# The last two blocks' input projection moved from behind dense 1 to inside it

## The chip, the cores and the metric

The kernel runs on one core of one Trainium2 chip. The metric is the time of one execution on the device in microseconds (us), as the median of several runs. PE is TensorE (matmuls), DVE is VectorE, ACT is ScalarE, POOL is GpSimd, and SP is the sync engine, which here issues most DMAs. PSUM is the memory into which PE accumulates; it has 8 banks of 128 x 512 fp32.

## The reference, cut to what matters

A state-space layer (S5) and a dense layer with mish read the same normalised input, and both results are added to the input:

```python
def _A_ref(x, Lambda_re, Lambda_im, B_re, B_im, C_re, C_im, log_dt, Dskip):
    Lam_bar = jnp.exp(dt * Lam)                                # dt = exp(log_dt)
    B_bar = ((Lam_bar - 1.0) / Lam)[:, None] * Bmat
    Bu = jnp.einsum("bld,pd->blp", x + 0j, B_bar)              # input projection
    for t in range(L):
        h = Lam_bar[None, :] * h + Bu[:, t, :]                 # recurrence
    y = 2.0 * jnp.einsum("blp,dp->bld", hseq, Cmat).real + x * Dskip[None, None, :]

def _B_ref(x, w1, b1, w2):
    h = jnp.einsum("bsd,df->bsf", x, w1) + b1                  # dense 1
    act = h * jnp.tanh(sp)                                     # sp = softplus(h): mish
    return jnp.einsum("bsf,fd->bsd", act, w2)                  # dense 2

xn = _layernorm(x, axis=-1)
return x + _A_ref(xn, ...) + _B_ref(xn, ...)
```

There are 2048 rows, 1024 columns and 1024 complex states, and 3584 hidden columns in the dense layer. Inputs and output are bf16.

## The kernel before, in words

The 2048 rows are cut into four blocks of 512 (`blk` 0 to 3 in the code; "blocks 3 and 4" of the change are `blk` 2 and 3, those with `blk >= FAST`). Rows 512 at a time stand in the free axis of `xnT`, the transposed normalised input. Each block goes through these stages on PE:

- **Dense 1**: 28 weight tiles `f`, each 8 matmuls of 512 columns (L777) into one PSUM bank, bank `f % 8`. DVE takes each tile out of its bank with one bias addition (L786) into `hb`. This is the tile's evacuation.
- **Input projection**: in `blk` 2 and 3 it is `project_fast`, a Strassen-like scheme with seven products for each of four pairs of state tiles, called `a` to `d`. A product (L830) is 8 matmuls of 256 columns. `ORDER` names products and what stands between them, in the order in which they are issued. For each pair the products use three banks X, Y and Z: 4, 5, 6 for `a` and `c`, and 0, 1, 2 for `b` and `d`. Products 1, 2 and 5 open a bank; 6, 7 and 4 add to what product 1 left in X, and 3 adds to what 5 left in Z. Before a bank is added to, its state has to be copied out. These copies ("snaps", L845 on DVE for `a` and `b`, L847 on ACT for `c` and `d`) go to SBUF, and additions of a bank and a snap ("joins", L855 on DVE) make the results. PE may issue `a6` only when DVE has done the snap of `a1`, `b6` only behind the snap of `b1`, and `a3` only behind the snap of `a5`. A last copy follows product 4 (L872 on DVE, L874 on ACT).
- **Dense 2 and output projection** (`tail`, both L956): eight accumulation units, one for each bank, take 28 hidden tiles and then the state tiles. In `blk` 2 and 3 the units 7, 5, 6 and 4 take the first six hidden tiles among the last products (the `u` entries in `ORDER`), as banks come free.

All instructions of an engine run in the order in which the Python code issues them. A helper (`Queue`) puts a semaphore wait in front of each instruction that reads or overwrites another engine's work.

Beside the stages run: on ACT the three passes of mish for each group of 7 tiles (`mish(g)`, L755 to L757), issued behind tiles 6, 13, 20 and 27; on DVE the product `mish_mul(g)` (L762), issued ahead of the evacuations of tiles 14 and 21 for groups 0 and 1, and at the `m` entries of `ORDER` for 2 and 3. Also on DVE: `ln_skip` behind tiles 8, 10, 12 and 15 (L516, L518); in `blk` 2 the eight calls of `sums_B` (four operations each, L1124 and L1126), which make the summed weights of the products; `rotate_in` (the `r` entries, L796 to L801); the layer norm of the next block; and `recur` (the recurrence). POOL makes the summed inputs with `sums_x` (L1131), each behind an `ln_skip`. SP loads weights into a ring of 7 slots (L375) as slots come free, and issues the transposes of the next block (L522), which are queued among the loads of dense 2.

Of the kernel before, what the change touches and what calls it, by code (L numbers as in the profile page):

```python
# [163 lines left out]
def build_kernel(nc, A_x, A_Lambda_re, A_Lambda_im, A_B_re, A_B_im, A_C_re, A_C_im,  # L164
# [6 lines left out]
    NB = S // TB  # L171
# [3 lines left out]
    NF = F // P  # L175
# [3 lines left out]
    assert S % TB == 0 and D == 1024 and NP == 1024 and NF == NG * GF and NQ == 4  # L179
    EPS = 1e-5  # L180
    FAST = 2

    PE = Queue(nc, "pe")
    VE = Queue(nc, "ve")
# [8 lines left out]
    NRING = 7  # L193
# [565 lines left out]
    def mish_mul(g):  # L759
        hs = hb[:, (g % 2) * GF:(g % 2) * GF + GF, :]  # L760
        a = act[:, g * GF:(g + 1) * GF, :]
        vop(lambda e: e.tensor_tensor(a, a, hs, op=ALU.mult), reads=[b_act[g], b_hb[g % 2]], writes=[b_act[g]])  # L762
# [6 lines left out]

    def first_tile(blk, f):  # L770
        bank, hs = f % 8, f % (2 * GF)
        raw = blk == 0 and f < NR
        if raw:
            first_rest(f)
        for k in range(0 if raw else NK):
            s, w = w1_tile(n_item[0], f % 4, k)
            PE.mm(lambda e, k=k, w=w: e.matmul(ps[:, bank, :], lhsT=w, rhs=xnT[:, k, :],  # L777
                                               start=k == 0, stop=k == NK - 1),
                  reads=[b_ring[s]] + b_xnT, writes=[b_ps[bank]], first=k == 0, last=k == NK - 1)
        if f % 4 == 3:  # L780
            item_done()
            item_done()
        if f % GF == 0 and f >= 2 * GF:
            mish_mul(f // GF - 2)
        ts = slice(2 * P if raw else 0, 4 * P)
        vop(lambda e: e.tensor_scalar(hb[:, hs, ts], ps[:, bank, ts], b1(f), None, op0=ALU.add),  # L786
            reads=[b_ps[bank], b_par], writes=[b_hbf[hs]])
        if f % GF == GF - 1:
            mish(f // GF)
# [4 lines left out]
    def rotate_in(j):  # L794
        for s in range(2):
            vop(lambda e, s=s: e.tensor_tensor(  # L796
                mt[:, s, :, :], hT16[:, :, j, :], tab[:, s, j, :].unsqueeze(1).to_broadcast([P, 2, TB]), op=ALU.mult),
                reads=[b_hT[0][j], b_hT[1][j], b_tab[j]], writes=[b_m[s]])
        vop(lambda e: e.tensor_tensor(hT[:, 0, j, :], mt[:, 0, 0, :], mt[:, 1, 1, :], op=ALU.add),
            reads=b_m, writes=[b_hT[0][j]])  # L800
        vop(lambda e: e.tensor_tensor(hT[:, 1, j, :], mt[:, 0, 1, :], mt[:, 1, 0, :], op=ALU.subtract),  # L801
            reads=b_m, writes=[b_hT[1][j]])
# [3 lines left out]
    def product(pr, n):  # L806

        X, Y, Z = (4 * ((pr + 1) % 2) + i for i in range(3))
        js = (2 * pr, 2 * pr + 1)
        lo, hi = slice(0, TH), slice(TH, TB)  # L810
        raw = {1: (0, 0, lo), 2: (0, NH, lo), 4: (1, NH, None), 3: (None, NH, hi)}
        bank = {1: X, 6: X, 7: X, 4: X, 2: Y, 5: Z, 3: Z}[n]
        opens = n in (1, 2, 5)
        for j in js:
            for k in range(NH):
                if n in (1, 2, 4):
                    w = BT[:, raw[n][0], j, raw[n][1] + k, :]
                    b_w = b_BT[j]
                elif n == 7:
                    w, b_w = BT16[:, 1, j, k, :], b_BT[j]  # L820
                else:
                    w, b_w = SS[:, j, {5: 0, 6: 1, 3: 2}[n], k, :], b_CT[j]
                if n in (1, 2, 3):
                    x, b_x = xnT[:, raw[n][1] + k, raw[n][2]], b_xnT
                else:
                    t = {5: 0, 6: 1, 7: 2, 4: 3}[n]
                    x, b_x = TT[:, t, k, :], [b_xn[t]]
                o = (j - js[0]) * TH
                begin, end = j == js[0] and k == 0, j == js[1] and k == NH - 1
                PE.mm(lambda e, w=w, x=x, o=o, begin=begin, end=end: e.matmul(  # L830
                    ps[:, bank, o:o + TH], lhsT=w, rhs=x, start=opens and begin, stop=end, skip_group_check=True),
                    reads=[b_w] + b_x, writes=[b_ps[bank]], first=begin, last=end, chained=not opens)

    def evacuate(pr, n, keep):
# [34 lines left out]
        if n == 4:  # L869
# [3 lines left out]
            else:  # L873
                aop(lambda e: e.copy(dst, bank(X)), reads=[b_ps[X]], writes=b_hT[1][j0:j0 + 2])  # L874

    ORDER = ("a2 a1 b2 b1 a5 b5 a6 b6 a3 b3 a7 b7 c2 d2 a4 b4 c5 c1 r0 d5 d1 r1 c6 c3 d6 d3 "
             "c7 d7 u7 c4 r2 u5 d4 u6 u4 r3 r4 r5 r6 r7 m2 m3")

    def project_fast(open_unit):
        keep = {}  # L880
        for o in ORDER.split():
            kind, n = o[0], int(o[1])
            if kind == "r":
                rotate_in(n)
            elif kind == "u":
                open_unit(n)
            elif kind == "m":
                mish_mul(n)
            else:
                product("abcd".index(kind), n)  # L890
                evacuate("abcd".index(kind), n, keep)

    def project_in(blk):
        for j in range(NJ):
# [55 lines left out]
    def tail(blk):  # L950
# [8 lines left out]
        def dense(f, s, units):  # L959
            wt = ring[:, s, :].rearrange("p (f d) -> p f d", f=2)  # L960
            for u in units:
                q, h = u // 2, u % 2
                acc(u, act[:, f, q * P:(q + 1) * P], wt[:, f % 2, h * TB:(h + 1) * TB], [b_actf[f], b_ring[s]],
                    tell=f % 2 == 1 and u == 7)

        base_items = [0]

# [17 lines left out]
        njt = 1 if blk == 0 else 3  # L985
        base = n_item[0]

        def open_unit(u):
            for f in range(6):
                dense(f, (base + f // 2) % NRING, (u,))  # L990

        yield open_unit
        if blk < FAST:
            for f in range(6):
                dense(f, (base + f // 2) % NRING, (4, 5, 6, 7))
        for f in range(NF):
            dense(f, (base + f // 2) % NRING, (0, 1, 2, 3) if f < 6 else range(8))
            if f % 2 == 1:
                item_done()
            if blk + 1 < NB and f in (9, 11, 13, 15):  # L1000
                transpose_dma((f - 9) // 2)
# [30 lines left out]
        for q in range(NQ):  # L1032
            units = (2 * q, 2 * q + 1) if not (ends and q == NQ - 1) else (2 * q,)
# [122 lines left out]
    for blk in range(NB):  # L1156
        def side(f):
            if blk:
                if f in (8, 10, 12, 15):
                    ln_skip(blk, (8, 10, 12, 15).index(f))  # L1160
                    if blk >= FAST:
                        sums_x((8, 10, 12, 15).index(f))
                if blk == FAST and f in (1, 2, 4, 5, 17, 19, 22, 24):
                    sums_B((1, 2, 4, 5, 17, 19, 22, 24).index(f))
                return
            if f == 13:
                for j in range(NJ):
                    table(j)
            if f in (5, 6, 7, 8):
                coefficients(f - 5)  # L1170
            if f in (8, 9, 11, 12):
                ln_skip(0, (8, 9, 11, 12).index(f))
            if f in (14, 16, 18, 20):
                ln_stats_only(1, (f - 14) // 2)
            if f < 24 and f % 3 == 2:
                transpose_B(f // 3)
            if f >= 26:
                transpose_C(f - 26)

        for f in range(NF):  # L1180
            first_tile(blk, f)
            side(f)
        out_stage = tail(blk)
        open_unit = next(out_stage)
        if blk >= FAST:
            project_fast(open_unit)
        else:
            project_in(blk)
        if 0 < blk < NB - 1:
            for q in range(NQ):  # L1190
                ln_stats_only(blk + 1, q)
            ln_rsqrt()
            for q in range(NQ):
                ln_scale(blk + 1, q)
        if blk:
            next(out_stage)
        for j in range(NJ):
            recur(blk, j)
            if blk == FAST - 1:
                prepare(j)  # L1200
            if blk:
                continue
            if j == 0:
                mish_mul(3)
                ln_root()
                for q in range(NQ):
                    ln_scale(1, q)
                next(out_stage)
            scale_C(j)
        if blk + 1 < NB:  # L1210
            carry()
        if blk == FAST - 1:
            vop(lambda e: e.tensor_tensor(qi[:], qi[:], c("ss").unsqueeze(1).to_broadcast([P, 2, NJ]), op=ALU.mult),
                reads=[b_qi, b_cs["ss"]], writes=[b_qi])
            rows_spread()
            for j in range(NJ):
                scale_B(j)
        for _ in out_stage:
            pass
        if blk == FAST - 1:  # L1220
            snaps_ready()
# [36 lines left out]
```

## Time and profile before

| What | Value |
|---|---|
| Time before, median of 3 runs (lowest, highest) | 614.18 us (614.16, 614.73) |
| The profiled execution: its own time | 614.87 us |
| Its span in the profile | 613.6 us |
| Granted TensorE clock | 1.0 in all slices |
| Busy: PE, DVE, ACT, POOL | 609.6, 502.2, 289.9, 83.3 us |
| Dense 1 of `blk` 2, of `blk` 3 begins | 313.94, 462.72 us |
| Products of `blk` 2, of `blk` 3 begin | 362.29, 511.06 us |

Times within the profile are counted from the start of the span. A line of a timeline gives the start, the length, the engine, the line of the kernel, the operation, output and input, the number of instructions that are merged into the line, and, in square brackets, the idle time in front of it and what ended it. "x3" with a length of 2.18 us is three instructions that followed each other without a pause; the distance of their starts is less than the length of one, because the end of one overlaps the next. The chain of waits is followed back from the last instruction of the kernel, and a piece of it gives start, length, engine and line.

### The profile page before, as it was taken

To read this page: it belongs to the slowest core of one execution; us is meant where nothing else is said; L and a number is where in the kernel's file an instruction comes from. 1 tells how busy PE (TensorE), PEld (TensorE's weight loads), DVE (VectorE), ACT (ScalarE), POOL (GpSimd) and SP (SyncE) were. 2 spreads that over 40 slices of the span, in tenths; PEclk is the share of its full clock that TensorE was granted. 3 is DMA by queue.
4 is the path that set the end of the run, shared out by engine and by line. 5 is a ranking of instruction groups with operands and counts; after the bars stand their busy time and mean duration, and the time that the engine had idled before them with its cause. 6 is when DMAs were issued, how large, how long until landed. Compare 5 with 4: busy or idle time off the path is not lost.

```text
span 613.6 us, 8046 instructions
## 1 busy us (share of the span) xinstructions
PE 609.6 (99%) x3151; PEld 306.9 (50%) x3151; DVE 502.2 (82%) x796; ACT 289.9 (47%) x217; POOL 83.3 (14%) x83
## 2 busy tenths in 40 slices
PE   8999999999999999999999999999999999999998
PEld 7644444444444444444444468544444447844444
DVE  6989999999557599999968886999954776799923
ACT  4589998332059952724605998000000999400000
POOL 2899200000100001300013300000000510000000
PEclk9999999999999999999999999999999999999999
DMA  9999984950355401997545530059446443016421
GB/s 233 291 246 301 222 166 133 259 158 0 117 160 171 170 2 52 308 296 223 237 139 160 181 138 1 1 177 275 160 140 209 138 152 123 1 41 235 170 71 69
DMA packets 102768, 97.02 MB, mean 158 GB/s; under 512 B 51722, under 2 KB 81034, under 8 KB 102730
## 3 DMA queue, kind: packets, MB, share of 16 engines
q1 hardware_dynamic: 96688, 80.56, 45.7%
q0 software_dynamic: 2352, 7.61, 3.9%
q10 hardware_dynamic: 3690, 8.34, 3.6%
q8 instruction: 25, 0.41, 0.3%
q14 instruction: 13, 0.11, 0.1%
HBM read 76.04 MB, written 8.39 MB: 138 GB/s over the span
## 4 chain that ended last, share of the span: by engine, by line
PE 98%; DMA 1%; SPq 0%; DVE 0%; issue 0%
PE ps L956 49%; PE ps L777 30%; PE ps L898 9%; PE ps L830 8%; PE ps L582 1%; PE ps L591 1%; DMA ring<-in_B_w_dram 1%; PE ps L981 0%; PE ps L434 0%; SPq L343 0%; PE ps L469 0%; DVE xx L1046 0%; SPq L339 0%; PE ps L617 0%
## 5 line engine op out<-in xcount | busy, mean ns | idle before, releaser
L956 PE MATMUL ps<-ring,act 128*128 128x512 bf16 x896 | 194.7, 379 | 0.0
L777 PE MATMUL ps<-xnT,ring 128*128 128x512 bf16 x840 | 182.0, 379 | 0.0
L956 PEld LDWEIGHTS ps<-ring,act 128*128 128x128 bf16 x896 | 87.7, 98 | 104.5
L777 PEld LDWEIGHTS ps<-xnT,ring 128*128 128x128 bf16 x840 | 82.2, 98 | 98.9
L755 ACT ACTIVATE act<-hb 128x3584 bf16<-128x3584 bf16 x16 | 50.9, 3183 | 125.7 <-DVE hb L786 125.5
L786 DVE TENSOR_SCALAR hb<-ps,par 128x512 bf16<-128x512 f32 (+1 forms) x112 | 79.2, 728 | 37.4 <-PE ps L777 36.5
L921 DVE TENSOR_TENSOR_SCAN hT<-cs,qi,hT 128x512 bf16<-128x512 f32 x48 | 58.9, 1268 | 0.0
L898 PE MATMUL ps<-xnT,BT 128*128 128x512 bf16 x256 | 55.6, 379 | 0.0
L956 PE MATMUL ps<-CT,hT 128*128 128x512 bf16 x256 | 55.6, 379 | 0.0
L956 PE MATMUL ps<-ring,hT 128*128 128x512 bf16 x250 | 54.3, 379 | 0.0
L757 ACT ACTIVATE act<-act 128x3584 bf16<-128x3584 bf16 x16 | 51.0, 3190 | 0.2
L756 ACT ACTIVATE act<-act 128x3584 bf16<-128x3584 bf16 x16 | 51.0, 3190 | 0.2
L926 DVE TENSOR_TENSOR mt<-hT,tab 128x1024 bf16<-128x1024 bf16 x64 | 41.4, 688 | 1.1
L903 DVE TENSOR_TENSOR mt<-ps,tab 128x1024 bf16<-128x1024 f32 x32 | 37.7, 1219 | 5.0 <-PE ps L898 3.9
L898 PEld LDWEIGHTS ps<-xnT,BT 128*128 128x128 bf16 x256 | 25.1, 98 | 30.2
L956 PEld LDWEIGHTS ps<-CT,hT 128*128 128x128 bf16 x256 | 25.0, 98 | 30.2
L956 PEld LDWEIGHTS ps<-ring,hT 128*128 128x128 bf16 x250 | 24.4, 98 | 29.5
L762 DVE TENSOR_TENSOR act<-act,hb 128x3584 bf16<-128x3584 bf16 x16 | 34.1, 2144 | 3.3 <-ACT act L757 3.3
L1023 DVE TENSOR_TENSOR xx<-ps,xx 128x1024 bf16<-128x1024 f32 (+1 forms) x16 | 18.8, 1189 | 22.0 <-PE ps L956 21.9
L1131 POOL TENSOR_TENSOR TT<-xnT 128x1024 f16<-128x1024 bf16 x4 | 10.3, 2582 | 146.7 <-DVE mt L516 146.7
L1077 ACT ACTIVATE hb<-hb 128x1024 bf16<-128x1024 bf16 x16 | 16.7, 1046 | 23.1 <-DMA hb<-in_A_B_re_dram 13.5
L1108 ACT ACTIVATE act<-CT,cs 128x2048 bf16<-128x2048 bf16 x7 | 14.0, 2002 | 22.1 <-DVE cs L1091 19.7
(142 smaller groups left out, 578.9 us busy)
## 6 DMA issues: line engine op xcount, KB each, us to landing
ring<-in_B_w_dram SPq DMA_DIRECT2D x112, 512.0 KB, 4.5
ring<-ctd SPq DMA_DIRECT2D x16, 512.0 KB, 3.2
out_dram<-xx ACTq DMA_DIRECT2D x15, 256.0 KB, 2.0
ctd<-act ACTq DMA_DIRECT2D x7, 512.0 KB, 3.8
xx<-in_A_x_dram POOLq DMA_DIRECT2D x12, 256.0 KB, 3.9
hb<-in_A_B_re_dram POOLq DMA_DIRECT2D x8, 256.0 KB, 4.0
hb<-in_A_B_im_dram POOLq DMA_DIRECT2D x8, 256.0 KB, 4.1
xx<-in_A_x_dram SPq DMA_DIRECT2D x3, 256.0 KB, 5.9
```

Source lines behind the costliest of these rows:

```text
L755: aop(lambda e: e.activation(a, hs, AF.Exp), reads=[b_hb[g % 2]], writes=[b_act[g]])
L756: aop(lambda e: e.activation(a, a, AF.Ln, bias=1.0), reads=[b_act[g]], writes=[b_act[g]])
L757: aop(lambda e: e.activation(a, a, AF.Tanh), reads=[b_act[g]], writes=[b_act[g]])
L762: vop(lambda e: e.tensor_tensor(a, a, hs, op=ALU.mult), reads=[b_act[g], b_hb[g % 2]], writes=[b_act[g]])
L777: PE.mm(lambda e, k=k, w=w: e.matmul(ps[:, bank, :], lhsT=w, rhs=xnT[:, k, :], start=k == 0, stop=k == NK - 1), reads=[b_ring[s]] + b_xnT, ...
L786: vop(lambda e: e.tensor_scalar(hb[:, hs, ts], ps[:, bank, ts], b1(f), None, op0=ALU.add), reads=[b_ps[bank], b_par], writes=[b_hbf[hs]])
L830: PE.mm(lambda e, w=w, x=x, o=o, begin=begin, end=end: e.matmul(ps[:, bank, o:o + TH], lhsT=w, rhs=x, start=opens and begin, stop=end, ski ...
L898: PE.mm(lambda e, j=j, ci=ci, k=k, bank=bank: e.matmul(ps[:, bank + ci, :], lhsT=BT[:, ci, j, k, :], rhs=xnT[:, k, :], start=k == 0, stop= ...
L903: vop(lambda e, s=s, u=u, j=j: e.tensor_tensor(mt[:, s, :, :], u, tab[:, s, j, :].unsqueeze(1).to_broadcast([P, 2, TB]), op=ALU.mult), rea ...
L921: vop(lambda e, ci=ci, init=init: e.tensor_tensor_scan(out=hT[:, ci, j, :], data0=cj("r", j).to_broadcast([P, TB]), data1=hT[:, ci, j, :], ...
L926: vop(lambda e, s=s: e.tensor_tensor(mt[:, s, :, :], hT[:, :, j, :], tab[:, s, j, :].unsqueeze(1).to_broadcast([P, 2, TB]), op=ALU.mult), ...
L956: PE.mm(lambda e: e.matmul(ps[:, u, :], lhsT=lhsT, rhs=rhs, start=st_, stop=last), reads=reads, writes=[b_ps[u]], first=st_, last=last, te ...
```

## The change

In `blk` 2 the products are issued behind dense 1's tile 21, in `blk` 3 behind tile 15 (`SPLIT` 22 and 16 counts the tiles ahead). Two tiles stand among the last products, the others behind them (`f` in `ORDER` and `REST`). All of dense 2 comes behind tile 27: the `u` entries are gone, and four units take the first six hidden tiles, then the other four. The tiles use banks in an order of their own. `mish_mul(3)` moves on DVE from the end of `ORDER` to behind the first state tile of `recur`. In `blk` 2 the last five calls of `sums_B` move to earlier tiles.

```diff
+    SPLIT = {blk: 22 if blk == FAST else 16 for blk in range(FAST, NB)}
...
     def first_tile(blk, f):
         bank, hs = f % 8, f % (2 * GF)
+        if blk >= FAST:
+            f0 = f - SPLIT[blk]
+            bank = (EARLY_BANKS if f0 < 0 else LATE_BANKS)[f0 % 8]
...
+    EARLY_BANKS = (5, 1, 4, 0, 6, 2, 3, 7)
+    LATE_BANKS = (7, 3, 5, 1, 6, 2, 4, 0)
     ORDER = ("a2 a1 b2 b1 a5 b5 a6 b6 a3 b3 a7 b7 c2 d2 a4 b4 c5 c1 r0 d5 d1 r1 c6 c3 d6 d3 "
-             "c7 d7 u7 c4 r2 u5 d4 u6 u4 r3 r4 r5 r6 r7 m2 m3")
-
-    def project_fast(open_unit):
+             "c7 d7 f c4 f d4 ")
+    REST = {16: "f r2 f f r3 f f r4 f f r5 f f f r6 r7 m2", 22: "f r2 f r3 f r4 f r5 r6 r7 m2"}
+
+    def project_fast(tile, f):
         keep = {}
-        for o in ORDER.split():
+        for o in (ORDER + REST[f]).split():
...
+            if kind == "f":
+                tile(f)
+                f += 1
...
             for u in units:
                 q, h = u // 2, u % 2
                 acc(u, act[:, f, q * P:(q + 1) * P], wt[:, f % 2, h * TB:(h + 1) * TB], [b_actf[f], b_ring[s]],
-                    tell=f % 2 == 1 and u == 7)
+                    tell=f % 2 == 1 and u == units[-1])
...
+        opens, rest = (4, 5, 6, 7), (0, 1, 2, 3)
+        if blk >= FAST:
+            opens, rest = ((7, 4, 3, 0), (5, 1, 6, 2)) if SPLIT[blk] == 22 else ((6, 2, 4, 0), (7, 3, 5, 1))
+        for f in range(6):
+            dense(f, (base + f // 2) % NRING, opens)
         for f in range(NF):
-            dense(f, (base + f // 2) % NRING, (0, 1, 2, 3) if f < 6 else range(8))
+            dense(f, (base + f // 2) % NRING, rest if f < 6 else range(8))
...
-                if blk == FAST and f in (1, 2, 4, 5, 17, 19, 22, 24):
-                    sums_B((1, 2, 4, 5, 17, 19, 22, 24).index(f))
+                if blk == FAST and f in (1, 2, 4, 6, 11, 14, 17, 19):
+                    sums_B((1, 2, 4, 6, 11, 14, 17, 19).index(f))
...
-        for f in range(NF):
+        def tile(f):
             first_tile(blk, f)
             side(f)
-        out_stage = tail(blk)
-        open_unit = next(out_stage)
+
+        for f in range(SPLIT.get(blk, NF)):
+            tile(f)
         if blk >= FAST:
-            project_fast(open_unit)
+            project_fast(tile, SPLIT[blk])
         else:
             project_in(blk)
+        out_stage = tail(blk)
...
-        if blk:
+        if 0 < blk < FAST:
             next(out_stage)
         for j in range(NJ):
             recur(blk, j)
+            if blk >= FAST and j == 0:
+                mish_mul(3)
+                next(out_stage)
```

More of the change, by code (lines that the diff above doesn't have):

```diff
@@ L874, in evacuate @@
                 aop(lambda e: e.copy(dst, bank(X)), reads=[b_ps[X]], writes=b_hT[1][j0:j0 + 2])
+    EARLY_BANKS = (5, 1, 4, 0, 6, 2, 3, 7)
+    LATE_BANKS = (7, 3, 5, 1, 6, 2, 4, 0)
     ORDER = ("a2 a1 b2 b1 a5 b5 a6 b6 a3 b3 a7 b7 c2 d2 a4 b4 c5 c1 r0 d5 d1 r1 c6 c3 d6 d3 "
-             "c7 d7 u7 c4 r2 u5 d4 u6 u4 r3 r4 r5 r6 r7 m2 m3")
-    def project_fast(open_unit):
+             "c7 d7 f c4 f d4 ")
+    REST = {16: "f r2 f f r3 f f r4 f f r5 f f f r6 r7 m2", 22: "f r2 f r3 f r4 f r5 r6 r7 m2"}
+    def project_fast(tile, f):
         keep = {}
-        for o in ORDER.split():
[L882 to L886, printed above, removed]
+        for o in (ORDER + REST[f]).split():
+            kind = o[0]
+            if kind == "f":
+                tile(f)
+                f += 1
+            elif kind == "r":
+                rotate_in(int(o[1]))
             elif kind == "m":
-                mish_mul(n)
+                mish_mul(int(o[1]))
             else:
-                product("abcd".index(kind), n)
-                evacuate("abcd".index(kind), n, keep)
+                product("abcd".index(kind), int(o[1]))
+                evacuate("abcd".index(kind), int(o[1]), keep)
+        assert f == NF
     def project_in(blk):
@@ L986, in tail @@
         base = n_item[0]
[L988 to L995, printed above, removed]
+        opens, rest = (4, 5, 6, 7), (0, 1, 2, 3)
[3 more added lines that the diff above has]
+            dense(f, (base + f // 2) % NRING, opens)
         for f in range(NF):
-            dense(f, (base + f // 2) % NRING, (0, 1, 2, 3) if f < 6 else range(8))
+            dense(f, (base + f // 2) % NRING, rest if f < 6 else range(8))
             if f % 2 == 1:
```

## The prediction

> **What bounds the kernel now.** I read the page's busy table first: PE is busy 609.6 of 613.6 us. Busy is not proof of full rate, so next came the chain of waits (start, length, engine and line):
>
> ```profile
> 313.94 48.35 PE ps L777 x224
> 362.29 22.71 PE ps L830 x208
> 385.00 1.29 PE ps L956 x6
> 386.29 0.87 PE ps L830 x8
> 387.17 1.29 PE ps L956 x6
> 388.46 0.87 PE ps L830 x8
> 389.33 73.38 PE ps L956 x340
> ```
>
> Each piece starts where the last one ends. A 512-column matmul costs 48.35/224 = 0.2158 us and a 256-column one 22.71/208 = 0.1092 us, in every piece of `blk` 2 and 3. So there is no hole in PE's stream to close. The change leaves every matmul in place and only reorders them: it can gain nothing on PE, and whatever makes PE wait is lost for good. The question is only whether PE must now wait for a bank, a snap or an activation.
>
> Next, DVE's timeline around the place where the products begin, and one SS group (`sums_B`) and one POOL operation ahead of it:
>
> ```profile
> 344.88 2.56 POOL L1131 TENSOR_TENSOR TT<-xnT,TT 128x1024 f16<-128x1024 bf16 x1 [4.39 <-DVE mt L516]
> ...
> 346.70 1.03 DVE L1124 TENSOR_TENSOR SS<-BT 128x512 f16<-128x512 bf16 x1
> 350.35 0.41 DVE L1124 TENSOR_TENSOR SS<-BT 128x512 f16<-128x512 bf16 x1
> 360.90 2.18 DVE L786 TENSOR_SCALAR hb<-ps,par 128x512 bf16<-128x512 f32 x3
> 364.07 0.69 DVE L845 COPY snaps<-ps 128x512 f32<-128x512 f32 x1 [0.99 <-PE ps L830]
> 364.80 0.69 DVE L855 TENSOR_TENSOR hT<-ps,snaps 128x512 f16<-128x512 f32 x1
> ```
>
> At tile 28 DVE has caught up and even waits 0.99 us for the first snap. But behind tile 21 (evacuated at 356.16, when PE had left it at about 351.9) DVE is over 4 us late. The new order starts the products exactly there. The same operation takes 1.03 us at 346.70 and 0.41 at 350.35: at 346.70 POOL's sum runs until 347.44, and DVE ends 0.29 later. In `blk` 3 a `mish_mul` shows it more strongly:
>
> ```profile
> 486.63 2.63 POOL L1131 TENSOR_TENSOR TT<-xnT 128x1024 f16<-128x1024 bf16 x1 [0.82 <-DVE mt L516]
> ...
> 487.86 3.29 DVE L762 TENSOR_TENSOR act<-act,hb 128x3584 bf16<-128x3584 bf16 x1
> 500.20 2.02 DVE L762 TENSOR_TENSOR act<-act,hb 128x3584 bf16<-128x3584 bf16 x1 [0.44 <-ACT act L757]
> ```
>
> It ends 1.89 us behind POOL's end (489.26): nearly its whole 2.02 us lie behind POOL. A DVE operation with two SBUF inputs thus waits until POOL's running sum is over.
>
> **The change, part by part. DVE in `blk` 2.** Nothing moves ahead of tile 10's evacuation (332.98) but the fourth SS group, from behind tile 5 to behind tile 6, into a hole of 0.53 us. From there I add DVE's queue up in its new order, by distances of starts in the trace: an evacuation 0.66 (two in 1.32 at 342.73 to 344.05), an `ln_skip` 1.33, an SS group 1.72, a `mish_mul` 2.13. An SS group caught behind POOL ends 1.58 after POOL's end (349.02 - 347.44), a `mish_mul` 1.99 after it (491.25 - 489.26). POOL's sum ends 4.05 us after the evacuation ahead of its `ln_skip` begins (332.98 to 337.03).
> - Tile 10 and skip: 334.97. Tile 11: 335.63. SS group 5, now here, meets POOL until 337.03: 338.61.
> - Tile 12 and skip: 340.60. POOL starts late too and runs to 342.67. Tile 13: 341.26. `mish_mul(0)` waits for POOL: 344.66.
> - Tile 14 and SS group 6: 347.04. Tile 15 and skip: 349.03, POOL until about 351.05. Tiles 16, 17: 350.35. SS group 7 waits for POOL: 352.63.
> - Tiles 18, 19 and SS group 8: 355.67. Tile 20: 356.33. `mish_mul(1)`: 358.46. Tile 21: **359.12**.
>
> None of this waits for PE or ACT: ACT's first mish ends at about 339, the second at 353.5 (12.1 us each by 328.37 to 340.47).
>
> **PE meets it.** Without stalls the products start at 313.94 + 22 x 1.727 = 351.93, one each 0.873: `a6` at 357.17, `b6` at 358.04, `a3` at 358.91. The six products ahead of `a6` need banks 5, 4, 1, 0, 6, 2, last used by tiles 14 to 19 and empty by 354: no wait. DVE's snaps follow tile 21 (0.73 for a snap with its join behind, 0.61 for the join, 0.65 for snaps in a row, a length of 0.69): snap `a1` ends 359.81, `b1` 361.15, `a5` 362.49. So with 0.06 for the signal (DVE's first operation ends at 0.98, PE starts at 1.04) `a6` starts at 359.87, 2.70 late; `b6` adds 0.47, `a3` 0.47. `a3` starts at 362.55 instead of 358.91: **3.64 us**. Behind it the line is clear: `a7` starts 0.5 us behind its snap, `c5` is ready at 370.4 and ACT's mish, begun at about 356.5, is over by 368.6.
>
> Each restart may also pay for a weight load; the rows give 98 ns, and only the last restart counts: 0.1 us, between 0 and 0.1.
>
> **The rest of `blk` 2.** PE ends tile 27 at T = 390.4. The last six evacuations stand among `r` entries; tile 27's ends at T + 3.8, needed at T + 5.8, when the second four units begin (24 matmuls ahead of them). `m2`: T + 12, needed at tile 14 of dense 2, T + 24. Then the layer norm (11.1 us by 402.75 to 413.85), one `recur` (4.5) and `mish_mul(3)` (2.1): T + 30; ACT's third pass is over at T + 16; needed at tile 21, T + 36. The next block's transposes wait on SP for the norm, until T + 23, in front of weight loads for tile 24 of dense 2 (T + 41); before, they were issued at 412.60 to 418.97, some 10 us ahead of that tile. All hidden, with 2 us of cover at the least; if one is late, PE pays what is over.
>
> **`blk` 3** has no SS groups. DVE's queue up to tile 15 is unchanged and ends with the skip at 493.90; products start at 490.35. Snap `a5` ends at 497.27, `a3` starts at 497.33: cover zero, cost 0 to 0.1; I take 0.05. Its two joins ahead fall in POOL's last sum (to 495.96); if they were held as above, `a3` would be 1.3 late. They read one input from PSUM, and L599, of that kind, keeps its 0.42 us at 19.23 with POOL busy, so I take 0. Behind tile 27 (T), its evacuation is done at T + 1.7, `m2` at T + 8, `mish_mul(3)` at T + 16: covered.
>
> Sum: 3.64 + 0.1 + 0.05 = 3.8 us. Against the profiled execution's own 614.87 (span 613.6 and 1.27 around it) that is 618.7; against the median, 0.69 lower, 618.0.
>
> **A clock penalty.** PE has never stood still for 2.7 us in this trace. The nearest rows: at the start 128-column matmuls run at 0.107 us (18 in 2 us) and only from 6.57 at 0.055, so the array runs at half rate in its first 5.5 us; a pause of 0.83 us at 7.07 does not bring that back (56 of 257 columns in 6.18 us, 0.110 each). So the price of the new pause lies between 0 and 5.5/2 = 2.75 us; I take 0, the row of the pause being of the same kind.
>
> The Trainium skill ("TensorE: Matmul & The Clock Gate", "Why this matters for your kernels") says that matmul bursts shouldn't lie more than about 3 us apart, or the array drops to half clock; no row here shows it. By that rule 2.70 us just passes and the sum stays 3.8; a stall 0.3 us longer would break it, so the rule speaks against this change.
>
> **The rivals.**
> 1. *DVE is not held by POOL* (the two long rows have another cause). Then tile 21 is out 3.1 us earlier, at 356.03; `a6` finds its snap done, `a3` starts 0.55 late: 614.18 + 0.55 + 0.1 = 614.8, no measurable change. Against it: both rows end by POOL's end, and four `mish_mul`s without POOL beside them take 2.02. Chance 0.10.
> 2. *The pause trips the clock*: 3.8 plus up to 2.75, less what later stalls (0.94) absorb: about 619 to 620.6. For it: 2.7 us is three times the longest pause shown. Chance 0.10.
> 3. *A later wait* (dense 2's second units, `mish_mul(3)`, or `blk` 3's joins): 0.5 to 2 us more, 618.5 to 620. For it: covers of 2 us and zero. Chance 0.09.
> 4. *Faster*: only if PE's stream held waits that the trace hides. At 0.2158 us for all 224 matmuls of a piece, a hidden stop has no room. Chance 0.02.
>
> The forecast itself, 617.3 to 618.6, has 0.69. A measurement of this kernel can tell about 0.2%, 1.2 us, from no change. Faster 0.02, same 0.10 (rival 1), slower 0.88. The range takes rivals 2 and 3 in, up to 620.6, and below it reaches to one of the three POOL waits (1.27, 1.26, 0.56) or two being absent: 618.0 - 2.2 = 615.8.
>
> **What would show it.** In the profile after: PE waits at L830 for DVE L845, three in `blk` 2, the longest about 2.7 us, some 3.6 in all; tile 21's evacuation ends near 359.2; SS groups 5 and 7 and `mish_mul(0)` stretched behind POOL; no PE wait in `blk` 3 over 0.1; the granted clock and 0.109 us for each product matmul unchanged. The prediction is wrong if `a6` starts by 358 or if waits appear at L956.

## The result, and the profile after

| | Kernel before | Changed kernel |
|---|---|---|
| Median (lowest to highest), 4 runs each | 614.34 us (614.16 to 614.73) | 619.59 us (618.12 to 621.16) |
| Ratio to before, 95% interval | | 1.0085 (1.0059 to 1.0111) |
| Profiled execution, its span | 614.87, 613.6 us | 620.03, 618.6 us |
| Mean granted clock | 1.0 | 0.997 in three of the four, 1.0 in the run of 618.12 |

The kernel became 5.25 us slower. The forecast was 618.0 us with a range from 615.8 to 620.6. The one run with an undisturbed clock took 618.12.

The chain of waits of the changed kernel (start, length, engine and line; L790, L763, L849 and L859 are before's L786, L762, L845 and L855, and L834 the products) shows where PE's unbroken stream of before is cut:

```profile
314.06 19.01 PE ps L781 x88
...
358.59 0.75 DVE hb L790
...
360.66 0.61 DVE snaps L849
361.27 0.05 issue
361.32 18.14 PE ps L834 x152
...
391.56 75.97 PE ps L965 x352
...
495.16 22.84 PE ps L834 x208
```

Before, the chain was PE alone from 22 us on. Now it leaves PE behind tile 10 (333.07) and runs through DVE's queue up to the snap of `b1`; only `b6`, at 361.32, takes it back. Two lengths are also new. The 152 product matmuls from there take 18.14 us, where 152 x 0.1092 is 16.60. And the 208 of `blk` 3 take 22.84 instead of 22.71: the 0.13 us at `a3`. Behind 391.56 all other pieces have before's lengths.

PE's timeline around the products, and its only wait behind the kernel's start in the waits (total, times, longest):

```profile
355.38 1.91 PE L834 MATMUL ps<-TT,SS 128*128 128x256 f16 x16
359.99 3.21 PE L834 MATMUL ps<-TT,SS 128*128 128x256 f16 x16 [2.70 <-DVE snaps L849]
```

```profile
PE ps L834 <- DVE snaps L849: 2.7, 1, 2.7
```

`a5` and `b5` take 1.91 us; PE stands still for 2.70; then `a6` and `b6`, of the same size, take 3.21 with one short wait for the snap of `b1` (in PE's row it is hidden behind the weight load, whose own row waits 0.56 us). The windows (PE, weight load, DVE, ACT and POOL busy, then the granted clock) say why:

```profile
core 0: us, PE busy (x) PEld busy (x) DVE busy (x) ACT busy (x) POOL busy (x), PEclk, DMA share, GB/s
...
357.20:359.90 2.70, 0.09 (x1) 0.00 (x0) 2.59 (x3) 2.68 (x2) 0.00 (x0) 1.00 0.00 0
359.90:361.00 1.10, 1.01 (x8) 0.70 (x8) 1.07 (x3) 1.10 (x1) 0.00 (x0) 0.89 0.00 0
361.00:362.00 1.00, 0.88 (x5) 0.50 (x5) 0.96 (x3) 0.99 (x2) 0.00 (x0) 0.50 0.00 0
...
364.00:365.00 1.00, 1.00 (x11) 0.84 (x10) 0.73 (x2) 0.98 (x2) 0.00 (x0) 0.92 0.00 0
```

The pause runs at full clock; 0.77 us behind it the clock drops to 0.50 (0.89 over 1.10 us: half for the last 0.24) and is back 0.16 us behind 364.00. That is 3.40 us of half rate.

DVE's timeline in the same stretch:

```profile
335.75 1.68 DVE L1130 TENSOR_TENSOR SS<-BT 128x512 f16<-128x512 bf16 x1
...
341.38 3.29 DVE L763 TENSOR_TENSOR act<-act,hb 128x3584 bf16<-128x3584 bf16 x1
...
350.46 1.02 DVE L1130 TENSOR_TENSOR SS<-BT 128x512 f16<-128x512 bf16 x1
...
356.47 2.01 DVE L763 TENSOR_TENSOR act<-act,hb 128x3584 bf16<-128x3584 bf16 x1
358.59 0.75 DVE L790 TENSOR_SCALAR hb<-ps,par 128x512 bf16<-128x512 f32 x1
```

POOL's timeline, with the three sums they meet:

```profile
334.59 2.56 POOL L1137 TENSOR_TENSOR TT<-xnT,TT 128x1024 f16<-128x1024 bf16 x1 [0.89 <-DVE mt L517]
340.15 2.63 POOL L1137 TENSOR_TENSOR TT<-xnT 128x1024 f16<-128x1024 bf16 x1 [3.00 <-DVE mt L517]
348.64 2.56 POOL L1137 TENSOR_TENSOR TT<-xnT,TT 128x1024 f16<-128x1024 bf16 x1 [5.86 <-DVE mt L517]
```

SS groups 5 and 7 and `mish_mul(0)` are stretched just where the prediction put POOL's sums (0.41 to 1.68 and 1.02, and 2.02 to 3.29): the SS operations end 0.28 us behind POOL's end, `mish_mul(0)` 1.89. Tile 21's evacuation begins at 358.59 and the snap behind it at 359.26. Summed in advance was 359.12, in a time that began 0.12 earlier.

### The profile page after: what moved, and what is told of

It is laid out like the page before. It is cut to its first block, busy times and chain, and to the rows that moved or that the text cites. A ratio compares the mean times of both kernels' runs of the same rounds, so it can differ in the third digit from the quotient of the medians.

```text
span 618.6 us, 8053 instructions
## 1 busy us (share of the span) xinstructions
PE 611.4 (99%) x3151; PEld 306.5 (50%) x3151; DVE 503.7 (81%) x796; ACT 290.6 (47%) x217; POOL 84.9 (14%) x83
## 4 chain that ended last, share of the span: by engine, by line
PE 94%; DVE 5%; DMA 1%; SPq 0%; issue 0%; DVEq 0%
PE ps L965 49%; PE ps L781 26%; PE ps L907 9%; PE ps L834 7%; DVE hb L790 1%; DVE SS L1130 1%; PE ps L583 1%; PE ps L592 1%; DMA ring<-in_B_w_dram 1%; DVE act L763 1%; DVE xx L519 0%; DVE mt L517 0%; DVE BT L1132 0%; PE ps L990 0%; DVE snaps L849 0%; PE ps L435 0%
## 5 line engine op out<-in xcount | busy, mean ns | idle before, releaser
L790 DVE TENSOR_SCALAR hb<-ps,par 128x512 bf16<-128x512 f32 (+1 forms) x112 | 79.5, 729 | 38.3 <-PE ps L781 37.3
L763 DVE TENSOR_TENSOR act<-act,hb 128x3584 bf16<-128x3584 bf16 x16 | 35.5, 2219 | 2.9 <-ACT act L758 2.9
L340 POOL DMA_DIRECT2D xx<-in_A_x_dram x12 | 6.7, 559 | 129.0 <-DVE xx L1029 124.6
```

## The experiments

The theory was: DVE's queue in `blk` 2, lengthened by SS groups put ahead of the products and by waits for POOL, is late with the snap of `a1`; PE stands still; and the pause trips the clock in some executions. The rivals were a cost of the move itself (late evacuations, `mish_mul(3)`, `blk` 3), and a clock or a scatter that has nothing to do with the pause.

The start of the kernel scatters. In these profiles `blk` 2 begins anywhere from 312.8 to 314.6 us (a wait of its own in e1 left out), behind code that no kernel here changes, and the kernel before takes 613.85 to 616.62 us over three sets of runs. So besides the times I give, as **loss in `blk` 2**, the distance from dense 1's first matmul to dense 2's first in PE's timeline, less 72.80 us for 224 matmuls of 0.2158 and 224 of 0.1092. For the changed kernel it is 391.40 - 313.90 - 72.80 = 4.70.

| Kernel | Median us | Before, run beside it | Ratio, 95% interval | Clock below 1.0 | Loss in `blk` 2 |
|---|---|---|---|---|---|
| a1_after_again | 620.15 | 614.20 | 1.0095 (1.0077 to 1.0112) | 5 of 6 | 4.55 |
| e11_fill_3 | 620.07 | 614.53 | 1.0092 (1.0078 to 1.0105) | 4 of 6 | 3.75, clock 1.0 |
| e6_fill_half | 618.40 | 614.20 | 1.0070 (1.0058 to 1.0082) | 0 of 5 | 3.78 |
| e2_fill_pause | 618.65 | 614.73 | 1.0064 (1.0052 to 1.0077) | 0 of 5 | 3.78 |
| e3_split24 | 616.56 | 614.73 | 1.0026 (1.0015 to 1.0037) | 0 of 7 | 1.63 |
| e5b_no_pool | 615.30 | 614.53 | 1.0017 (1.0008 to 1.0025) | 0 of 12 | 0.61 |
| e8_split26_reordered | 614.98 | 614.53 | 1.0008 (0.9997 to 1.0019) | 0 of 10 | 0.01 |
| e7_blk3_alone | 614.76 | 614.20 | 1.0010 (0.9999 to 1.0021) | 0 of 12 | |
| e1_blk3_only | 617.22 | 614.73 | 1.0037 (1.0024 to 1.0051) | 0 of 5 | own waits |
| e4_split26 | 624.16 | 614.73 | 1.0149 (1.0135 to 1.0163) | 4 of 4 | own waits |

### Which block pays

**e1_blk3_only.** `blk` 2 is put back behind all 28 tiles, but inside the new code:

```diff
-    SPLIT = {blk: 22 if blk == FAST else 16 for blk in range(FAST, NB)}
+    SPLIT = {2: 28, 3: 16}
...
-                if blk == FAST and f in (1, 2, 4, 6, 11, 14, 17, 19):
+                if blk == FAST and f in (1, 2, 4, 5, 17, 19, 22, 24):
```

> In blk 2 the products stand behind all 28 tiles again and the SS groups at their old tiles; blk 3 is as in the changed kernel. Theory (the whole loss is DVE's late queue in blk 2 and the clock after PE's pause): 614.3 to 614.6 us, executions as close together as those of the kernel before, no PE wait for a snap in blk 2, at most 0.15 us at a3 of blk 3. Rival (the new order costs something in blk 3 too, in dense 2's units or mish_mul(3)): 615 us or more, with PE waits behind 460 us.

Neither came true as meant: 2.5 us were lost, and two waits that this version brought with it, 1.41 and 0.81 us in `blk` 2, make most of it. PE's timeline:

```profile
315.45 1.89 PE L781 MATMUL ps<-xnT,ring 128*128 128x512 bf16 x8 [1.41 <-DVE xx L1029]
```

```profile
387.47 1.92 PE L834 MATMUL ps<-TT,BT 128*128 128x256 f16 x16 [0.81 <-DVE hT L859]
```

With 28 as the split, the bank list gives tile 0 bank 6, which the block before frees last. And without tiles (or, in the old code, `u` units) between `d7` and `c4`, `c4` comes before DVE has joined `c7`. It undoes the change only in name, so it says nothing on `blk` 3.

**e7_blk3_alone** restores the old order of `blk` 2 with its banks and units (`project_old` goes through the `ORDER` of before):

```diff
+    SPLIT = {3: 16}
...
-        if blk >= FAST:
+        if blk in SPLIT:
             project_fast(tile, SPLIT[blk])
+            out_stage = tail(blk)
+        elif blk >= FAST:
+            out_stage = tail(blk)
+            project_old(next(out_stage))
...
```

> blk 2 exactly as in the kernel before (its order with the u entries, its banks, its mish_mul(3) and its SS tiles), blk 3 as in the changed kernel; e1 had waits of its own in blk 2. Theory (blk 3's move costs only the 0.13 us at a3): 0 to 0.3 us above before, no PE wait behind 20 us longer than 0.15. Rival (blk 3's move has a cost of its own): 1 us or more above before.

The median is 0.56 us above before, over the 0.3 expected, with an interval that reaches from nothing to 1.3. No product waits in its list of PE's waits, and the products of `blk` 3 take 22.84 us as in the changed kernel. So 0.13 us is what the profile gives to `blk` 3; the median can neither confirm nor exclude a few tenths.

### How much DVE's queue costs

**e3_split24** moves `blk` 2's products two tiles back:

```diff
-    SPLIT = {blk: 22 if blk == FAST else 16 for blk in range(FAST, NB)}
+    SPLIT = {2: 24, 3: 16}
...
```

> The changed kernel with blk 2's products behind tile 23 instead of 21. Theory (PE gains 1.727 us with each tile ahead of the products, DVE loses 0.66): DVE ends tile 23's evacuation 1.3 us later, PE wants a6 3.45 us later; a6 waits 0.55 us, the chain to a3 1.5 us in all; 615.8 to 616.1 us, clock 1.0 in every execution since no pause exceeds 0.6 us. Rival (the loss hangs on the tiles that now stand behind the products, as late evacuations in dense 2): a loss in proportion to the tiles moved, 4 of 6: about 617 us.

```profile
361.04 1.05 PE L834 MATMUL ps<-TT,SS 128*128 128x256 f16 x8 [0.56 <-DVE snaps L849]
362.36 1.05 PE L834 MATMUL ps<-TT,SS 128*128 128x256 f16 x8 [0.28 <-DVE snaps L849]
```

The wait at `a6` is 0.56 against 0.55 expected. The loss in `blk` 2 is 1.63 against 1.5; the median rose by 1.83, and at 616.56 it lies above the 616.1 expected and below the rival's 617. The loss decides: four late tiles of six cost less than half of what six cost (3.75 at full clock, below), so it goes with DVE's lag, not with the tiles moved.

**e4_split26** goes two more tiles back (`SPLIT = {2: 26, 3: 16}`).

> The changed kernel with blk 2's products behind tile 25, the SS groups at the new tiles. Theory: DVE's snap of a1 ends at 362.5 us and a6 is wanted at 364.1, so PE waits for nothing in blk 2: 614.3 to 614.6 us, clock 1.0. Rival (the earlier SS groups or mish_mul(3)'s new place cost PE time wherever the products stand): 615.5 us or more.

A miss, and the slowest of all: 9.4 us above before. No snap is waited for any more, but with this split the last tile, 27, stands ahead of `d4`. So ACT's queue has the mish of tiles 21 to 27 ahead of its copy of `d4`, and dense 2 waits for that copy (ACT's timeline, then PE's):

```profile
386.51 3.19 ACT L756 ACTIVATE act<-hb 128x3584 bf16<-128x3584 bf16 x1 [1.93 <-DVE hb L790]
...
398.61 0.57 ACT L878 CAST hT<-ps 128x512 f16<-128x512 f32 x1
```

```profile
399.32 3.15 PE L965 MATMUL ps<-ring,act 128*128 128x512 bf16 x7 [6.93 <-ACT hT L878]
```

**e8_split26_reordered** keeps the split of 26 and puts tile 27 behind `d4`:

```diff
+    REST = {16: "f r2 f f r3 f f r4 f f r5 f f f r6 r7 m2", 26: "f r2 r3 r4 r5 r6 r7 m2"}
...
+        for o in ((ORDER if f < 26 else ORDER.replace("f d4 ", "d4 ")) + REST[f]).split():
```

> As e4 (blk 2's products behind tile 25, SS groups at the changed kernel's tiles), but tile 27 comes behind d4, so that ACT's copy of d4 isn't queued behind the mish of tiles 21 to 27. Theory: DVE has caught up by tile 25 and PE waits for nothing in blk 2; with blk 3's 0.13 us, 0 to 0.5 us above before, no PE wait for a snap over 0.1 in blk 2, clock 1.0. Rival (the earlier SS groups or the tiles behind the products cost PE time by themselves): 1 us or more above before.

PE's timeline has no wait among the products, and the loss in `blk` 2 is 0.01 us. The SS groups' early tiles, the new banks, `mish_mul(3)` and dense 2 behind the tiles cost nothing that the profile shows, once the products stand four tiles later, DVE has caught up and ACT's order is right. It is not faster than before either: PE had nothing to give.

### Who makes DVE late

**e5b_no_pool** leaves POOL's sums out of `blk` 2; the products read the transposed input in their place, so the kernel's results are not the reference's:

```diff
+        raw_in = n_prod[0] < 28
+        n_prod[0] += 1
...
+                    if raw_in:
+                        x, b_x = xnT[:, NH * (t // 2) + k, TH * (t % 2):TH * (t % 2) + TH], b_xnT
...
-                    if blk >= FAST:
+                    if blk > FAST:
                         sums_x((8, 10, 12, 15).index(f))
```

> In blk 2 POOL's four sums are left out and the products read the transposed input itself in their place, so the values of blk 2 are not those of the reference. DVE's and PE's instructions keep their number, sizes and order. Theory (DVE's operations with two SBUF inputs wait for POOL's running sum, 3.1 us in all): SS groups 5 and 7 take 1.72 us each and mish_mul(0) 2.0, tile 21's evacuation ends about 3.1 us earlier, near 356.1 plus the start's scatter, a6 and b6 wait for nothing or 0.1, a3 starts 0.55 late; 0.6 to 0.9 us above the kernel before, clock 1.0. Rival (the three were long for another reason, such as their place): no difference from the changed kernel, 3.7 us or more above before.

DVE's timeline shows the same instructions at their short lengths, and PE's one remaining wait:

```profile
335.28 0.41 DVE L1136 TENSOR_TENSOR SS<-BT 128x512 f16<-128x512 bf16 x1
...
339.63 2.02 DVE L763 TENSOR_TENSOR act<-act,hb 128x3584 bf16<-128x3584 bf16 x1
...
354.95 0.75 DVE L790 TENSOR_SCALAR hb<-ps,par 128x512 bf16<-128x512 f32 x1
```

```profile
359.00 1.92 PE L840 MATMUL ps<-xnT,SS 128*128 128x256 bf16 x16 [0.28 <-DVE snaps L855]
```

Tile 21's evacuation begins 358.59 - 354.95 = 3.64 us earlier, of which 0.48 is the earlier start (tile 10's: 332.62 and 333.10): 3.16, with 3.1 expected. The loss falls to 0.61, the median to 0.77 above before. So of 3.75 us, 3.1 are DVE's waits for POOL. The new order without them costs 0.6. (An earlier version, e5_pool_short, which cut POOL's sums to 16 of 256 columns, gave no time.)

### What the clock adds

**a1_after_again** is the changed kernel once more, beside the others.

> The changed kernel itself, for its scatter beside the others on this chip. Theory (a pause of 2.70 us trips the clock in some executions and not in others, by where it falls in a free-running window): executions at clock 1.0 lie 3.6 to 4 us above the kernel before, those with one window of half clock (0.997) another 1 to 3 us above, so 618 to 621.5 in all. Rival (the first profile was a chance): all at 618.

Its six executions: 618.11 at clock 1.0, and 619.33, 619.75, 620.55, 620.73 and 622.19 at 0.997. The last lies above the 621.5 expected.

**e2_fill_pause** gives PE work for the pause:

```diff
+                if o == "a6" and SPLIT[FAST] == 22 and f == 22:
+                    for i in range(12):
+                        PE.mm(lambda e: e.matmul(ps[:, 3, :], lhsT=xnT[:, 0, 0:P], rhs=xnT[:, 0, :], start=True, stop=True),
+                              reads=b_xnT, writes=[b_ps[3]], first=i == 0, last=i == 11)
                 product("abcd".index(kind), int(o[1]))
```

> The changed kernel with 12 more matmuls of 512 columns (2.59 us, their result is not used) between b5 and a6 of blk 2, where PE otherwise stands still for 2.70 us. Theory (the pause is DVE's, and the time above 618.1 comes from the clock that halves because of the pause): the matmuls cost nothing, since PE would wait anyway; 618.1 us, granted clock 1.0 in every execution, executions within 0.7 us of each other. Rival (the scatter from 618.1 to 621.2 comes from something else, or the clock halves on DVE's late snaps whatever PE does): the same scatter as the changed kernel, clock 0.997 in most. Rival (PE doesn't really wait there): 620.7 us, 2.6 more than 618.1.

Twelve more matmuls make the kernel 1.3 to 2.0 us faster than the changed one (3.92 us above before against 5.25 and 5.95). Its executions lie within 0.90 us, where 0.7 was expected and the kernel before, run beside it, has 1.83, and the clock is 1.0 in all. Neither DVE nor its late snaps are touched: the pause itself is what costs the clock.

**e6_fill_half** has `range(6)` in their place and leaves 1.4 us of pause; **e11_fill_3** has `range(3)` and leaves 2.0.

> The changed kernel with 6 more matmuls of 512 columns ahead of a6, so that PE's pause is 1.4 us and not 2.7. Theory (the clock is halved when a window of fixed length, 3.4 us in the first profile after, is idle for most of it): 3.6 to 4.2 us above before, clock 1.0 in every execution. Rival (a pause over about 1 us is enough): 0.997 in some executions, and up to 3 us more.

> The changed kernel with 3 more matmuls of 512 columns ahead of a6: PE's pause is 2.05 us (2.70 tripped the clock in 8 of 10 executions, 1.4 in none of 5). Theory (a window of 3.41 us that is idle for more than about half trips it; the pause falls on it at random): some executions at 0.997, about half, and some at 1.0. Rival (the pause has to fill nearly a whole window, or the count of late snaps decides): all at 1.0, or 8 of 10 at 0.997 as without the matmuls.

PE's timelines, of e6 and of e11:

```profile
358.90 1.05 PE L834 MATMUL ps<-TT,SS 128*128 128x256 f16 x8 [1.41 <-DVE snaps L849]
```

```profile
359.08 1.05 PE L834 MATMUL ps<-TT,SS 128*128 128x256 f16 x8 [2.04 <-DVE snaps L849]
360.40 1.05 PE L834 MATMUL ps<-TT,SS 128*128 128x256 f16 x8 [0.27 <-DVE snaps L849]
361.72 1.92 PE L834 MATMUL ps<-xnT,SS 128*128 128x256 bf16 x16 [0.28 <-DVE snaps L849]
363.48 1.91 PE L834 MATMUL ps<-TT,BT 128*128 128x256 f16 x16
```

A pause of 1.41 us tripped the clock in none of 5 executions, one of 2.04 in 4 of 6, one of 2.70 in 8 of 10 (the changed kernel's two sets). The 1.41 us that PE waits in e1 tripped it in none of 5 either. The expectation's "about half" for 2.04 holds, but 4 of 6 can't be told from its rival's 8 of 10. Three more profiles with an untouched clock (e2, e6, e11) agree on a loss in `blk` 2 of 3.75 to 3.78; the two with half clock have 4.70 and 4.55, so a window of half clock cost 0.8 to 0.95 there. At 3.40 us long it could cost 1.70; the rest was taken from the waits of `b6` and `a3`, which shrink when PE is slower.

Open: the slowest executions. 622.19 is 4.1 us above 618.11, more than one window can cost, and e11 has one of 621.57 at clock 1.0. They were not profiled, and a mean clock of 0.997 leaves no room for a second window: half clock for 3.41 of some 620 us makes 0.997, two windows 0.995. The two profiled executions at 0.997 do add up: from before's 614.87, `blk` 2 begins 0.12 and 0.85 us later, the losses are 4.70 and 4.55 and 0.13 in `blk` 3, and 0.16 and 0.36 more lie outside the span, 619.98 and 620.76 for 620.03 and 620.73 measured. The kernel before scatters by up to 2.1 us above its median as well (616.62 against 614.53), which may be the rest of the slowest ones.

## Why the prediction was right, and what in it was wrong

- **PE has nothing to gain: right.** Every piece of before's chain comes back with its length, and the version without any wait (e8) is not faster than before (1.0008, 0.9997 to 1.0019).
- **DVE's queue: right.** Summed to 359.12 us for tile 21; 359.25 measured (358.59 and 0.66), of which 0.12 is the later start.
- **The stall of 3.64 and 0.1 us: right in the sum, in part by luck.** It was 3.75 to 3.78 in the three profiles with a full clock, but two slips in the sum nearly cancel (below).
- **POOL holds DVE: right.** Rival 1 had 0.10 and 614.8 us; e5b is the same sum as a kernel, and came to 0.77 above before where that rival has 0.65.
- **`blk` 3: right in the profile.** 0.05 was taken and 0.13 measured; with the slip of 0.16 us (below) put right, its sum gives 0.16. The joins beside POOL's last sum were not held: the first takes 0.69 us from 499.44, with POOL at work from 498.22 to 500.79. The row it was argued from did not show this: in the profile before, L606, which has both inputs in SBUF, keeps its 0.42 at 19.57 beside the same POOL work (L601) as L599 does at 19.23, so that row tells the two cases apart in nothing. The Trainium skill ("SBUF — State Buffer", "SBUF: two separate sides") says that GpSimd and VectorE share a port pair that one instruction takes whole, and counts only VectorE operations with two SBUF inputs or in a two-port mode; the joins' second input is in PSUM. Row and rule agree here.
- **The cover behind tile 27: right.** `m2` ends at T + 11.8 with T + 12 summed, `mish_mul(3)` at T + 29.3 with T + 30, T being 391.56.
- **The clock: wrong.** The step that failed is "I take 0, the row of the pause being of the same kind". A pause of 0.83 us was the nearest row, but it was far off: a pause of 2.70 trips the clock in 8 of 10 executions. So rival 2, which had 0.10, was the likeliest case, and its 619 to 620.6 holds both medians (619.59 and 620.15). The likeliest time should have been 619 to 620 and not 618.0: the measured 619.59 lies outside the 617.3 to 618.6 that had 0.69, and inside the range only because that took rival 2 in. The Trainium skill's limit ("TensorE: Matmul & The Clock Gate", "Why this matters for your kernels") is a pause of about 3 us; these runs show trips from 2.04 us on, so the measurement decides. The chance, not the price, was off: the cost in the two profiles, 0.8 to 0.95 us, lies within the 0 to 2.75 that the rows gave, and the later stalls did absorb part of it.

A slip in the same step: the 56 matmuls in 6.18 us have 256 columns, not 257, and begin 8 us behind the pause. The 16 of 257 columns right behind it take 1.96 us, 0.12 each, where 0.107 for 128 columns would make 0.21. So the row still shows that the pause of 0.83 us did not bring half rate back.

The two slips in the stall: the prediction took PE's starts from the chain, where dense 1 of `blk` 2 begins at 313.94, and DVE's from the timeline, where before's row of dense 1 is

```profile
313.78 48.51 PE L777 MATMUL ps<-xnT,ring 128*128 128x512 bf16 x224
```

So PE wanted `a6` 0.16 us earlier than summed, and 3.64 should have been 3.80. By starts `a6` is 2.87 late in the changed kernel: 359.99 against 313.90 and 43.22 for 176 matmuls of 0.2158 and 48 of 0.1092. The 2.70 in its row is counted from the end of `b5`; that it equals the 2.70 of the sum is chance. On the other side, the 0.1 for a weight load at the last restart isn't in the rows: in e11 16 matmuls from `a3` on take 363.48 - 361.72 = 1.76, and 16 x 0.1092 is 1.75.

## What to carry to other kernels

When one engine is busy without a hole, a new order can gain nothing on it and may lose: add up the queue of the engine that has to hand over first at the new meeting point, its waits for a third engine included. In that sum a piece of work moved ahead can cost more than its length, since it may start while another engine holds what it needs; here 3.1 of 3.75 us were such waits. And a stall is not over when the engine restarts: a pause of 2 us or more may cost TensorE a stretch of half clock, so matmuls whose result nobody uses, put into the pause, can make a kernel faster, as the twelve of e2 did.

## What the runs showed of the hardware

The clock is judged in windows of fixed length, as far as three profiles show it: the half clock lasted 3.40 us in the changed kernel (above), and in its second profile from 0.65 over 1.30 us to 0.74 over 1.00:

```profile
358.00:360.70 2.70, 0.02 (x1) 0.00 (x0) 2.56 (x3) 2.68 (x2) 0.00 (x0) 1.00 0.00 0
360.70:362.00 1.30, 1.27 (x8) 0.85 (x8) 1.29 (x2) 1.29 (x2) 0.00 (x0) 0.65 0.00 0
362.00:364.00 2.00, 2.00 (x11) 1.37 (x10) 1.97 (x4) 2.00 (x1) 0.00 (x0) 0.50 0.00 0
364.00:365.00 1.00, 1.00 (x9) 0.81 (x7) 1.00 (x2) 1.00 (x1) 0.00 (x0) 0.74 0.00 0
```

That is 0.91 + 2.00 + 0.52 = 3.43 us. In e4, where PE stands still from 392.4 to 399.3, the clock is 0.78 over these 6.90 us, 0.50 over the next 2.70 and 0.73 over the 2.00 behind: 3.04 + 2.70 + 1.08 = 6.82 us of half clock, two such windows. There the drop comes inside the pause, 3.9 us behind its beginning.

In the other two profiles the drop comes 0.77 and 0.4 us behind the end of the pause, at no fixed distance. If the window ahead of the drop is as long, the pause lay inside it in both, to within 0.1 us, and in e4 PE stood still for all of it. An estimate from that, loose since it rests on ten executions: if a window trips when it is idle for more than some limit, and a pause of 2.70 us falls on windows of 3.41 at random, 8 trips in 10 put the limit at about 1.7 us, half a window. By this limit 2.04 us would trip 6 in 10 and 1.41 never; 4 of 6 and 0 of 5 were seen.
